# Token sums moved ahead of the switch from a feed-forward to a mixture of experts, on one core

## The chip, the cores and the metric

The kernel runs on one core of a Trainium2 chip. The metric is the device time of one execution in microseconds (us). TensorE is called PE below, VectorE DVE, ScalarE ACT, GpSimd POOL, and SyncE (which issues most DMAs) SP. PEld is the weight load of a PE matmul.

## The reference

A linear attention over 2 x 768 tokens with 8 heads of 48 gives x (1536 x 384). Two layers follow:

```python
h = x @ w_in                                  # 384 -> 2048
g = np.where(h > 0.0, h, np.exp(np.minimum(h, 0.0)) - 1.0)
x = g @ w_out                                 # 2048 -> 384
p = domain_probs / (domain_probs.sum(-1, keepdims=True) + 1e-09)
out = np.zeros((N, D))
for e in range(4):                            # four experts, each 384 -> 1024 -> 384
    out += p[:, e:e + 1] * (np.maximum(x @ w1[e], 0.0) @ w2[e])
```

## The kernel before

All matmuls are made in three passes over operands that are split into a rounded part ("hi") and a remainder ("lo", what the rounding left): hi x hi, hi x lo, lo x hi. Whoever makes an operand for PE therefore makes two: ACT writes hi, and DVE or POOL subtracts it from the full value for lo. A matmul is 128 x 128 by 128 x 512.

**Feed-forward.** The 2048 hidden columns are worked in 48 steps, n = 12 q + 4 block + f, over four quarters q, three blocks of 512 tokens and four groups of 128 columns f. Step n is a set of tokens in a hand-written list, ORDER: `h` (nine matmuls into one PSUM bank, and two ACT operations on it), `e` (DVE reads that bank, line 365, and ACT makes hi), `el` (lo, by DVE for `elnD`, by POOL for `elnP`, line 146 as all remainders of `sub`), `z` (nine matmuls into three banks). After the fourth f, `dr` adds the three banks to x2 (DVE, line 386), and in the last quarter ACT and POOL make hi and lo of x from x2 at once. So dr39 finishes token block 0 of x, dr43 block 1 and dr47 block 2.

**Experts.** The first product of the experts has 16 units of weights (an expert and a pair of its 128-column groups). Units 0 and 1 are made plainly (`plain`, line 564, 12 groups of nine matmuls), from x as it is. Units 2 to 15 take 15 products each in place of 18 (`product`, line 536): sums of token blocks times sums of weight blocks, a bilinear scheme. The sums of weight blocks are made by POOL (`sum_blocks`, line 451) for each unit, six operations, and split by `split_hi` (ACT) and `split_lo` (POOL). The token operands are made once: `sum_tokens` (DVE, line 516, sums of 512-column pieces of x2), then `tokens_hi` (ACT, line 519) and `tokens_lo` (DVE at line 524 where the sign is turned, POOL at line 146 otherwise), which write over places of x that are used up, or into xb. Each product's bank is read by `taken` (DVE line 548, or ACT) into results; chains of products add onto one bank. The hidden values of a group are split by `hidden_hi` (ACT, line 576) and `hidden_lo` (DVE, line 579), and `second` (line 587) multiplies them by the second weights; `weighted` and `added` finish the output.

**The order.** `experts` puts every operation down with a key, and they are emitted in the order of the keys; each engine works its own operations off strictly in that order. A key unit is one piece of three matmuls. The row of pieces is: 36 plain pieces (keys 0 to 35), then 210 products and 288 pieces of `second`, mixed. The end of ORDER (from the sign | on) is put down in front of it with negative keys: an `h` or `z` counts 3. At key 0 the switch closes the pools of the feed-forward (its 8 PSUM banks too) and opens those of the experts: 5 banks for chains and 3 for `second`. Before, all token sums lie behind the switch:

```python
for i, t in enumerate(TOKENS):
    at(1.2 + 1.1 * i, sum_tokens, *t)
...
    k = max(1.9 + 1.1 * made, free + 0.3 + 0.9 * (PLACE[r] // 3))
    at(k, tokens_hi, r)
    at(k + 0.7, tokens_lo, r)
```

The last tokens of ORDER before are "z43 el44D dr43D el39D h45 z44 e45 z39 el45P dr39A e46 h47 z45 el46D z46 e47 el47D z47 dr47A", in the order of PE's parts.

Of the kernel before, what the change touches and what calls it, by code (L numbers as in the profile page):

```python
# [32 lines left out]
TERMS = 18  # L33
EDGE = 120


# [8 lines left out]
HEADS = {0, 6, 3, 9, 14}  # L45
MINUS = {6, 4, 12, 8, 5, 1, 0, 9, 2}

LOADED = [(0, 0), (1, 0), (0, 1), (1, 2), (0, 2), (1, 1)]
W0, W3, W1, W5, W2, W4 = range(5, 11)
SLOT = {11: 0, 0: 1, 8: 2, 9: 3, 14: 4, 7: W0, 2: W3, 3: W2, 6: W4, 4: 11, 10: 12, 13: 13, 5: 14, 12: 15, 1: 16}  # L50

SUMS = [((SLOT[13], SLOT[5]), (W1, W5), "-", (W0, W3)), ((SLOT[4], SLOT[12]), (SLOT[13],) * 2, "-", (W4, SLOT[5])),
        ((SLOT[9], SLOT[10]), (W2, SLOT[5]), "-", (W5, W2)), ((SLOT[11], SLOT[1]), (SLOT[4], SLOT[10]), "+", (W3, W0)),
        ((SLOT[0], SLOT[8]), (W1, W5), "-", (W4, W4)), ((SLOT[14],), (W2,), "-", (W1,))]
PLACE = dict(zip(TURNS, [9, 10, 11, 12, 13, 14, 0, 3, 6, 1, 4, 7, 2, 5, 8]))

TOKENS = [("q", (1, 1), (2, 1)), (0, "q", (0, 1)), (6, (1, 2), None), (3, (2, 2), None), (4, 0, (1, 2)), (7, 4, (0, 2)),
# [3 lines left out]

# [29 lines left out]
def kernel_body(ctx, tc, wkr, vv, uu, w_in, w_out, w1, w2, dp, out):  # L91
# [7 lines left out]
    def feed_forward_pools(es):  # L99
        for name, bufs in (("wpool", 4), ("stage", 4), ("hpool", 3)):  # L100
            pools[name] = es.enter_context(tc.tile_pool(name=name, bufs=bufs))
        pools["psum"] = es.enter_context(tc.tile_pool(name="psum", bufs=8, space=PSUM))

    def bank():
        return pools["psum"].tile([P, 512], F32, tag="bank", name="bank")

    m1 = ExitStack()
    feed_forward_pools(m1)
# [308 lines left out]
    def late_pools(es):  # L417
        for name, bufs in (("w2", 2), ("terms", TERMS), ("hl", 4), ("shares", 4), ("scaled", 4), ("guard", 1)):
            pools[name] = es.enter_context(tc.tile_pool(name=name, bufs=bufs))
        for name, bufs in (("chain", 5), ("second", 3)):  # L420
            pools[name] = es.enter_context(tc.tile_pool(name=name, bufs=bufs, space=PSUM))

    def experts(guard=False, lead=(), switch=None):

        events = []

        def at(key, run, *args):
# [80 lines left out]

        def sum_tokens(name, a, c):
            def of(i):  # L510
                return x2[:, i[0], 512 * i[1]:512 * i[1] + 512] if isinstance(i, tuple) else full[i]
            if c is None:
                full[name] = of(a)
            else:
                full[name] = term()
                nc.vector.tensor_tensor(full[name], of(a), of(c), ALU.add)  # L516
# [4 lines left out]
        def tokens_lo(r):  # L521
            hi, lo = (tokens(r)[:, m] for m in range(2))
            if r in MINUS:
                nc.vector.scalar_tensor_tensor(lo, full[r], -1.0, hi.bitcast(F32), ALU.mult, ALU.subtract)
            else:
                sub("P", lo, full[r], hi)

# [3 lines left out]
        def product(u, r):  # L531
            c = CHAIN[r]
            if r in HEADS:
                banks[c] = pools["chain"].tile([P, 512], F32, tag="chain", name=f"chain_{c}")
            for i, (sa, sm) in enumerate(PASSES):
                nc.tensor.matmul(banks[c], lhsT=weights(u, r, sa), rhs=tokens(r)[:, sm],  # L536
                                 start=r in HEADS and i == 0, stop=i == 2, skip_group_check=True)

        def taken(u, r):
# [10 lines left out]
            if r in (0, 6, 3, 5, 8):  # L550
                copy("A", new({0: 0, 6: 5, 3: 2, 5: 3, 8: 4}[r]), ps)
            elif r == 13:
                op(new(1), ps, y(0), ALU.subtract)
            else:
                o, sign = {4: (2, "-"), 7: (2, "+"), 10: (5, "r"), 12: (0, "-"), 1: (0, "-"), 11: (3, "+"), 9: (3, "r"),
                           14: (1, "+"), 2: (5, "-")}[r]
                a, b = (ps, y(o)) if sign == "r" else (y(o), ps)
                op(y(o), a, b, ALU.add if sign == "+" else ALU.subtract)

        def plain(f, b, j):  # L560
            if j == 0:
                banks["p"] = pools["chain"].tile([P, 512], F32, tag="chain", name="chain_p")
            for i, (sa, sm) in enumerate(PASSES):
# [17 lines left out]
        def second(h, b, f, d):  # L581
            if f == 0:
                k = "chain" if h == 7 and b == 1 else "second"
                sums[d] = pools[k].tile([P, 512], F32, tag=k, name=k)
            w = w2s[h].rearrange("p s (f d) -> p s f d", f=4)
# [46 lines left out]
        row = [("plain", f, b, j) for b in range(3) for f in range(4) for j in range(3)]  # L632
        done = 0
        for n in range(210):
            row.append(("product", 2 + n // 15, TURNS[n % 15]))
            while done < 6 * (n + 1) // 5:
                row.append(("second",) + seconds[done])
                done += 1
# [19 lines left out]
        for e in range(4):  # L658
            for b in range(3):
                at(max(0, place["second", 2 * e, b, 0, 0] - 60), load_share, e, b)  # L660
        for u in range(16):
            n = place["product", u, 0] if u > 1 else -20 + 10 * u
            at(n - 75, load_blocks, u)
            if u < 2:
                for i in (0, 3):
                    at(n - 20 + i, split_hi, u, 0, 5, 6, i, 3)
                    at(n - 19 + i, split_lo, u, 0, 5, 6, i, 3)
                continue
            for i, s in enumerate(SUMS):
                at(n - 50 + 2 * i, sum_blocks, u, *s)  # L670
            for part, first, size, k in ((0, 9, 8, n - 34), (1, 0, 7, n - 14)):
                for i in (0, 4):
                    at(k + i, split_hi, u, part, first, size, i, min(4, size - i))
                    at(k + i + 1.4, split_lo, u, part, first, size, i, min(4, size - i))
        for h in range(8):
            n = place["second", h, 0, 0, 0]
            for m in range(2):
                at(n - 70 + m, load_second, h, m)
                for q in range(2):
                    at(max(0, n - 38 + 6 * m + 3 * q), second_hi, h, m, q)  # L680
                    at(max(0, n - 37 + 6 * m + 3 * q), second_lo, h, m, q)
        for i, t in enumerate(TOKENS):
            at(1.2 + 1.1 * i, sum_tokens, *t)
        for i, r in enumerate(TURNS):
            made = next(j for j, t in enumerate(TOKENS) if t[0] == r)
            free = {0: 11.5, 1: 23.5, 2: 35.5}.get(PLACE[r] % 3, 0) if PLACE[r] < 9 else 0
            k = max(1.9 + 1.1 * made, free + 0.3 + 0.9 * (PLACE[r] // 3))
            at(k, tokens_hi, r)
            at(k + 0.7, tokens_lo, r)
        if guard:  # L690
# [50 lines left out]
    with tc.If(some > 0, preferred_fallthrough_block=False):  # L741
        with ExitStack() as es:
# [80 lines left out]
```

## Time and profile before

| | us |
|---|---|
| runs shown: 679.7, 681.62, 681.14; median | 681.14 |
| profiled execution, device time | 681.25 |
| its span, first to last instruction | 679.4 |
| PE busy in the span | 643.0 |
| DVE busy | 493.6 |
| POOL busy | 403.2 |
| ACT busy | 305.7 |

The profiled execution lies 0.1 us above the median. Device time is its span and 1.85 us around it. The switch lies at about 290 us of the span; the part from there to the end is the experts.

### The profile page before, as it was taken

To read this page: it belongs to the slowest core of one execution; us is meant where nothing else is said; L and a number is where in the kernel's file an instruction comes from. 1 tells how busy PE (TensorE), PEld (TensorE's weight loads), DVE (VectorE), ACT (ScalarE), POOL (GpSimd) and SP (SyncE) were. 2 spreads that over 40 slices of the span, in tenths; PEclk is the share of its full clock that TensorE was granted. 3 is DMA by queue.
4 is the path that set the end of the run, shared out by engine and by line. 5 is a ranking of instruction groups with operands and counts; after the bars stand their busy time and mean duration, and the time that the engine had idled before them with its cause. 6 is when DMAs were issued, how large, how long until landed. Compare 5 with 4: busy or idle time off the path is not lost.

```text
span 679.4 us, 9111 instructions
## 1 busy us (share of the span) xinstructions
PE 643.0 (95%) x3314; PEld 523.8 (77%) x3314; DVE 493.6 (73%) x686; ACT 305.7 (45%) x584; POOL 403.2 (59%) x345
## 2 busy tenths in 40 slices
PE   6977999999999999997999999999999999999994
PEld 4766778888888877874788878878878788788773
DVE  7799998638564753599785787777877868777763
ACT  1334646657565654656444343524443434333220
POOL 5699776435331462787654577765876776744342
PEclk7689999999999999999899999999999999999997
DMA  7575661223202210110202122112130121300012
GB/s 261 163 218 163 189 214 47 69 63 93 70 24 69 78 41 25 69 47 0 86 24 86 32 70 70 39 30 89 40 101 16 40 69 46 103 0 1 0 47 98
DMA packets 20970, 50.83 MB, mean 75 GB/s; under 512 B 2680, under 2 KB 3880, under 8 KB 20916
## 3 DMA queue, kind: packets, MB, share of 16 engines
q1 hardware_dynamic: 20772, 50.15, 23.8%
q8 instruction: 28, 0.46, 0.3%
q14 instruction: 26, 0.21, 0.1%
q10 hardware_dynamic: 144, 0.00, 0.0%
HBM read 46.58 MB, written 2.38 MB: 72 GB/s over the span
## 4 chain that ended last, share of the span: by engine, by line
PE 76%; DVE 12%; POOL 4%; issue 3%; DMA 2%; ACT 2%; SPq 1%; DVEq 0%; POOLq 0%; ACTq 0%
PE second L587 24%; PE bank L357 13%; PE bank L377 12%; PE chain_a L536 8%; PE chain_b L536 5%; PE chain_c L536 3%; DVE terms L516 3%; PE chain_d L536 2%; PE bank L278 2%; PE bank L285 2%; DVE scaled L596 2%; DVE terms L548 1%; PE chain_e L536 1%; PE bank L329 1%; DVE w2s L146 1%
## 5 line engine op out<-in xcount | busy, mean ns | idle before, releaser
L587 PE MATMUL second<-hl,w2s 128*128 128x512 f32 x828 | 223.4, 391 | 4.4 <-DVE hl L579 2.1
L587 PEld LDWEIGHTS second<-hl,w2s 128*128 128x128 f32 x828 | 155.8, 188 | 38.1 <-DVE hl L579 2.4
L601 POOL TENSOR_TENSOR x<-scaled,x 128x512 f32<-128x512 f32 x60 | 84.9, 1437 | 96.1 <-DVE scaled L596 96.1
L146 POOL TENSOR_TENSOR sums<-blocks,sums 128x512 fp32r<-128x512 f32 (+1 forms) x60 | 83.3, 1397 | 36.4 <-ACT sums L150 36.4
L357 PE MATMUL bank<-x,w 128*128 128x512 f32 x432 | 104.1, 391 | 0.4 <-DVE e L365 0.4
L377 PE MATMUL bank<-hl,w 128*128 128x512 f32 x432 | 104.1, 391 | 0.1
L357 PEld LDWEIGHTS bank<-x,w 128*128 128x128 f32 x432 | 80.5, 188 | 18.5 <-DVE e L365 1.4
L377 PEld LDWEIGHTS bank<-hl,w 128*128 128x128 f32 x432 | 80.5, 188 | 17.7 <-POOL hl L146 0.9
L579 DVE SCALAR_TENSOR_TENSOR hl<-terms,hl 128x512 fp32r<-128x512 f32 x96 | 87.6, 916 | 8.0 <-ACT hl L576 7.9
L451 POOL TENSOR_TENSOR blocks<-blocks 128x256 f32<-128x256 f32 x84 | 69.4, 837 | 1.1
L146 POOL TENSOR_TENSOR hl<-e,hl 128x512 fp32r<-128x512 f32 x26 | 35.3, 1361 | 56.2 <-ACT hl L150 56.1
L576 ACT ACTIVATE hl<-terms 128x512 fp32r<-128x512 f32 x96 | 58.1, 624 | 16.3 <-PE chain L587 6.1
L365 DVE SCALAR_TENSOR_TENSOR e<-e,bank 128x512 f32<-128x512 f32 x48 | 32.4, 681 | 40.7 <-ACT e L361 40.7
L536 PE MATMUL chain_a<-x,sums 128*128 128x512 f32 x210 | 60.1, 395 | 1.6 <-DVE terms L548 1.6
L548 DVE TENSOR_TENSOR terms<-terms,chain_a 128x512 f32<-128x512 f32 x42 | 28.7, 683 | 40.0 <-PE chain_a L536 40.0
L150 ACT ACTIVATE sums<-blocks 128x512 fp32r<-128x512 f32 (+1 forms) x60 | 35.4, 593 | 42.2 <-PE chain_b L536 24.9
L150 ACT ACTIVATE terms<-chain_b 128x512 f32<-128x512 f32 x28 | 16.8, 598 | 83.7 <-PE chain_b L536 83.7
L536 PEld LDWEIGHTS chain_a<-x,sums 128*128 128x128 f32 x210 | 39.2, 189 | 11.6 <-DVE terms L548 3.7
L150 ACT ACTIVATE hl<-e 128x512 fp32r<-128x512 f32 x48 | 30.1, 629 | 36.4 <-PE bank L377 24.8
L596 DVE TENSOR_TENSOR scaled<-second,pr 128x512 f32<-128x512 f32 x60 | 39.3, 680 | 5.8 <-PE second L587 5.8
L360 ACT ACTIVATE e<-bank 128x512 f32<-128x512 f32 x48 | 28.4, 592 | 26.3 <-PE bank L357 13.4
L150 ACT ACTIVATE terms<-chain_a 128x512 f32<-128x512 f32 x28 | 16.7, 596 | 48.6 <-PE chain_a L536 48.6
(119 smaller groups left out, 1022.2 us busy)
## 6 DMA issues: line engine op xcount, KB each, us to landing
kr<-in_wkr SPq DMA_DIRECT2D x12, 512.0 KB, 3.9
raw<-in_w_in SPq DMA_DIRECT2D x16, 384.0 KB, 3.6
raw<-in_w_out SPq DMA_DIRECT2D x16, 384.0 KB, 3.2
blocks<-in_w SPq DMA_DIRECT2D x16, 384.0 KB, 3.3
raw<-in_w SPq DMA_DIRECT2D x16, 384.0 KB, 4.3
v<-in_vv SPq DMA_DIRECT2D x12, 456.0 KB, 4.0
w<-in_wkr SPq DMA_DIRECT2D x12, 258.5 KB, 3.8
gw<-in_wkr SPq DMA_DIRECT2D x12, 258.0 KB, 2.8
```

Of the source, the lines that this page charges most:

```text
L146: engines[e].tensor_tensor(o, a, b.bitcast(F32), ALU.subtract)
L150: nc.scalar.activation(out=o, in_=a, func=AF.Copy)
L357: nc.tensor.matmul(ph, lhsT=wi[:, sa, f, kk, :], rhs=x[:, kk, c0:c0 + nch, sm], start=(kk == 0 and i == 0), stop=(kk == 2 and i == 2))
L377: nc.tensor.matmul(pxs[q, bl][d], lhsT=wo[:, sa, f, d * P:(d + 1) * P], rhs=b["t"][:, sm], start=(f == 0 and i == 0), stop=(f == 3 and i = ...
L451: nc.gpsimd.tensor_tensor(*(places(blocks[u], p) for p in (r, a, c)), ALU.subtract if op == "-" else ALU.add)
L536: nc.tensor.matmul(banks[c], lhsT=weights(u, r, sa), rhs=tokens(r)[:, sm], start=r in HEADS and i == 0, stop=i == 2, skip_group_check=True)
L548: nc.vector.tensor_tensor(out, a, b, o)
L576: nc.scalar.activation(out=hls[f, b][:, 0], in_=results[f, b], func=AF.Relu)
L579: nc.vector.scalar_tensor_tensor(hls[f, b][:, 1], results[f, b], 0.0, hls[f, b][:, 0].bitcast(F32), ALU.max, ALU.subtract)
L587: nc.tensor.matmul(sums[d], lhsT=w[:, sa, f, d * P:(d + 1) * P], rhs=hls[4 * h + f, b][:, sm], start=f == i == 0, stop=f == 3 and i == 2)
L596: nc.vector.tensor_tensor(o, sums[d], prs[h // 2, b], ALU.mult)
L601: (nc.vector if last else nc.gpsimd).tensor_tensor(x2[:, d, s], scaled[d], x2[:, d, s], ALU.add)
```

## The change

- TOKENS loses the three entries that only passed a block of x2 on (6, 3 and 14, AS_IS): products 6, 3 and 14 read hi and lo of x as they stand, so `tokens_hi` and `tokens_lo` of these three are gone. Signs (MINUS) are arranged anew, with the signs in `taken` and the sums of weights to match.
- Ten of the sixteen sums that are left (q, 0, s0, 8, s2, v, 9, 12, 1, 11; those that need only token blocks 0 and 1) get the keys -15.5 to -4.7, within the last h and z of the feed-forward, into a pool of their own of 8 buffers; hi and lo of 0, 8, 9, 12, 1 and 11 follow them there. The other six have the keys 0.5 to 6. `tokens_lo` is POOL's for 8, 9 and 12 and DVE's for the other nine.
- The third unit's weights (u = 2): sums at keys -18 to -8 (before -14 to -4), the first half's split from -3 (before 2), the second half's at 32 (before 22). For all units the second half is split 4 keys later, and slots change so that its first user is the ninth product of a unit.
- Six pieces of `second` are put ahead of the first product (AHEAD), which moves that from key 36 to 42; from the thirtieth product on the row is as before.
- The tail of ORDER is changed so that dr39 and dr43 come three h and four z before the switch, with all the `el` there on DVE.
- One pool of 8 PSUM banks serves all stages. The pools of shares, scaled and guard open at key 8 where the ten sums lay, and the first two DMAs of shares move from key 0 to key 9.

```diff
+AHEAD = 6
+SPREAD = 8
-MINUS = {6, 4, 12, 8, 5, 1, 0, 9, 2}
+MINUS = {0, 13, 11, 5, 1}
-SLOT = {11: 0, 0: 1, 8: 2, 9: 3, 14: 4, 7: W0, 2: W3, 3: W2, 6: W4, 4: 11, 10: 12, 13: 13, 5: 14, 12: 15, 1: 16}
+SLOT = {12: 0, 1: 1, 11: 2, 9: 3, 8: 4, 14: 5, 2: W3, 3: W2, 6: W4, 7: W0, 0: 12, 4: 13, 10: 14, 13: 15, 5: 16}
...
+AS_IS = {6: (1, 2), 3: (2, 2), 14: (2, 1)}
+PLACE = {0: 9, 8: 10, 9: 11, 12: 12, 1: 13, 11: 14, 4: 0, 7: 3, 10: 6, 13: 1, 5: 4, 2: 2}
+TOKENS = [("q", (1, 1), (2, 1)), (0, "q", (0, 1)), ("s0", (0, 0), (0, 1)), (8, (1, 0), (1, 1)), ("s2", (2, 0), (2, 1)),
+          ("v", 8, "s2"), (9, "v", "s0"), (12, 8, (2, 1)), (1, 12, "s0"), (11, 12, (0, 1)),
+          (4, 0, (1, 2)), (7, 4, (0, 2)), (10, 9, (2, 2)), (13, "q", (1, 2)), (5, "v", (2, 2)), (2, 10, (0, 2))]
...
-z37 h44 wc31P el42P el43P el38D z41 h39 e44 e39 z42 h46 z38 z43 el44D dr43D el39D h45 z44 e45 z39 el45P dr39A e46 h47
-z45 el46D z46 e47 el47D z47 dr47A
+z37 h39 wc31P el42P el43P el38D z41 e39 h44 z42 z38 e44 el39D z39 el44D dr39D z43 dr43D h45 e45 h46 el45D z44 e46 h47
+el46D z45 e47 z46 el47D z47 dr47A
...
-        for name, bufs in (("w2", 2), ("terms", TERMS), ("hl", 4), ("shares", 4), ("scaled", 4), ("guard", 1)):
+        for name, bufs in (("w2", 2), ("terms", TERMS), ("hl", 4)):
-        for name, bufs in (("chain", 5), ("second", 3)):
-            pools[name] = es.enter_context(tc.tile_pool(name=name, bufs=bufs, space=PSUM))
+    def last_pools(es):
+        for name, bufs in (("shares", 4), ("scaled", 4), ("guard", 1)):
...
+            if r in AS_IS:
+                k, b = AS_IS[r]
+                return x[:, k, 4 * b:4 * b + 4].rearrange("q n s c -> q s n c")
...
-                banks[c] = pools["chain"].tile([P, 512], F32, tag="chain", name=f"chain_{c}")
+                banks[c] = pools["psum"].tile([P, 512], F32, tag="bank", name=f"chain_{c}")
...
-                op(new(1), ps, y(0), ALU.subtract)
+                nc.vector.scalar_tensor_tensor(new(1), ps, -1.0, y(0), ALU.mult, ALU.subtract)
...
+        row += [("second",) + g for g in seconds[:AHEAD]]
...
-                at(n - 50 + 2 * i, sum_blocks, u, *s)
-            for part, first, size, k in ((0, 9, 8, n - 34), (1, 0, 7, n - 14)):
+                at(n - (50 if u > 2 else 60) + 2 * i, sum_blocks, u, *s)
+            for part, at_first, size, k in ((0, 9, 8, n - (34 if u > 2 else 45)), (1, 0, 7, n - 10)):
...
-            at(1.2 + 1.1 * i, sum_tokens, *t)
...
+            made[t[0]] = -15.5 + 1.2 * i if i < 10 else 0.5 + 1.1 * (i - 10)
+            at(made[t[0]], sum_tokens, i < 10, *t)
+        for r, n in PLACE.items():
+            k = max(made[r] + 0.7, {0: 11.5, 1: 23.5, 2: 35.5}[n % 3] + 0.9 * (n // 3) if n < 9 else -99)
             at(k, tokens_hi, r)
-            at(k + 0.7, tokens_lo, r)
+            at(k + 0.9, tokens_lo, "P" if r in (8, 9, 12) else "D", r)
...
+        at(SPREAD, spread_out)
```

## Rows read from the trace of the kernel before

**Rows 1.** Page, part 1 and part 5 (busy, mean ns of one).

```profile
PE 643.0 (95%) x3314; PEld 523.8 (77%) x3314; DVE 493.6 (73%) x686; ACT 305.7 (45%) x584; POOL 403.2 (59%) x345
...
L548 DVE TENSOR_TENSOR terms<-terms,chain_a 128x512 f32<-128x512 f32 x42 | 28.7, 683 | 40.0 <-PE chain_a L536 40.0
```

**Rows 2.** Stretches: length, busy PE, PEld, DVE, ACT, POOL, PE clock, DMA, GB/s.

```profile
270.00:290.00 20.00, 19.85 (x87) 15.78 (x85) 10.61 (x15) 10.93 (x19) 14.37 (x13) 1.00 0.24 79
...
310.00:320.00 10.00, 7.69 (x30) 5.47 (x30) 10.00 (x9) 7.36 (x15) 9.61 (x8) 1.00 0.00 1
320.00:330.00 10.00, 7.18 (x23) 5.56 (x24) 8.06 (x8) 7.50 (x15) 10.00 (x8) 0.83 0.41 144
...
400.00:450.00 50.00, 49.37 (x217) 39.99 (x216) 38.61 (x55) 19.27 (x36) 37.43 (x34) 1.00 0.17 50
```

**Rows 3.** What PE waited for, 230 to 380 us: total, times, longest.

```profile
PE second L587 <- DVE hl L579: 2.1, 1, 2.1
PE chain_p L564 <- ACT terms L150: 1.8, 2, 1.3
PE second L587 <- ACT hl L576: 1.4, 1, 1.4
PE chain_p L564 <- DVE x L386: 0.8, 1, 0.8
```

**Rows 4.** Stretches of 1 us, columns as in Rows 2.

```profile
323.00:324.00 1.00, 0.69 (x3) 0.60 (x4) 1.00 (x2) 1.00 (x3) 1.00 (x1) 0.98 0.00 0
324.00:325.00 1.00, 1.00 (x4) 0.80 (x3) 1.00 (x2) 0.75 (x2) 1.00 (x3) 0.50 0.00 0
...
327.00:328.00 1.00, 1.00 (x5) 0.77 (x5) 0.24 (x1) 0.21 (x1) 1.00 (x1) 0.81 1.05 409
```

**Rows 5.** Timeline of DVE, 290 to 324 us: start, length, operation.

```profile
293.31 1.78 DVE L516 TENSOR_TENSOR terms<-x 128x512 f32<-128x512 f32 x1
...
298.27 0.68 DVE L524 SCALAR_TENSOR_TENSOR x<-terms,x 128x512 fp32r<-128x512 f32 x1
298.87 0.68 DVE L524 SCALAR_TENSOR_TENSOR x<-x,x 128x512 fp32r<-128x512 f32 x1
...
314.08 1.23 DVE L516 TENSOR_TENSOR terms<-terms 128x512 f32<-128x512 f32 x1
```

**Rows 6.** Timeline of POOL, 290 to 324 us.

```profile
296.19 1.74 POOL L146 TENSOR_TENSOR sums<-blocks,sums 128x512 fp32r<-128x512 f32 x1
...
313.57 3.48 POOL L451 TENSOR_TENSOR blocks<-blocks 128x256 f32<-128x256 f32 x3
```

**Rows 7.** Timeline of POOL, 273 to 291 us.

```profile
277.96 3.80 POOL L146 TENSOR_TENSOR x<-x,x 128x512 fp32r<-128x512 f32 x3
...
288.36 2.93 POOL L451 TENSOR_TENSOR blocks<-blocks 128x256 f32<-128x256 f32 x4
```

**Rows 8.** The chain that ended last, 260 to 400 us: start, length.

```profile
267.11 2.05 PE bank L377 x9
```

**Rows 9.** Timeline of DVE, 273 to 291 us.

```profile
273.96 2.05 DVE L386 TENSOR_TENSOR x<-bank,x 128x512 f32<-128x512 f32 x3 [3.40 <-PE bank L377]
...
278.65 0.69 DVE L365 SCALAR_TENSOR_TENSOR e<-e,bank 128x512 f32<-128x512 f32 x1 [1.53 <-ACT e L361]
```

**Rows 10.** Timeline of PE, 268 to 292 us.

```profile
271.04 4.24 PE L377 MATMUL bank<-hl,w 128*128 128x512 f32 x18
275.12 2.20 PE L357 MATMUL bank<-x,w 128*128 128x512 f32 x9
```

**Rows 11.** Timeline of ACT, 273 to 291 us.

```profile
277.36 0.60 ACT L360 ACTIVATE e<-bank 128x512 f32<-128x512 f32 x1
277.99 0.63 ACT L361 ACTIVATE e<-e 128x512 f32<-128x512 f32 x1
```

**Rows 12.** What PE waited for, 380 to 680 us.

```profile
PE chain_a L536 <- DVE terms L548: 1.6, 5, 0.3
...
PE second L587 <- DVE scaled L596: 0.9, 1, 0.9
```

More of the change, by code (lines that the diff above doesn't have):

```diff
@@ L417, in late_pools @@
     def late_pools(es):
-        for name, bufs in (("w2", 2), ("terms", TERMS), ("hl", 4), ("shares", 4), ("scaled", 4), ("guard", 1)):
+        for name, bufs in (("w2", 2), ("terms", TERMS), ("hl", 4)):
             pools[name] = es.enter_context(tc.tile_pool(name=name, bufs=bufs))
-        for name, bufs in (("chain", 5), ("second", 3)):
-            pools[name] = es.enter_context(tc.tile_pool(name=name, bufs=bufs, space=PSUM))
+    def last_pools(es):
+        for name, bufs in (("shares", 4), ("scaled", 4), ("guard", 1)):
+            pools[name] = es.enter_context(tc.tile_pool(name=name, bufs=bufs))
     def experts(guard=False, lead=(), switch=None):
         events = []
+        first, last = ExitStack(), ExitStack()
+        pools["first"] = first.enter_context(tc.tile_pool(name="first", bufs=8, side="right"))
         def at(key, run, *args):
@@ L507, in term, with sum_tokens, tokens_lo @@
             return pools["terms"].tile([P, 512], F32, tag="terms", name="terms")
-        def sum_tokens(name, a, c):
+        def sum_tokens(early, name, a, c):
             def of(i):
                 return x2[:, i[0], 512 * i[1]:512 * i[1] + 512] if isinstance(i, tuple) else full[i]
[L512 to L516, printed above, removed]
+            full[name] = pools["first"].tile([P, 512], F32, tag="first", name="first") if early else term()
+            nc.vector.tensor_tensor(full[name], of(a), of(c), ALU.add)
         def tokens_hi(r):
             nc.scalar.activation(out=tokens(r)[:, 0], in_=full[r], func=AF.Copy, scale=-1.0 if r in MINUS else 1.0)
-        def tokens_lo(r):
+        def tokens_lo(e, r):
             hi, lo = (tokens(r)[:, m] for m in range(2))
@@ L525, in tokens_lo @@
             else:
-                sub("P", lo, full[r], hi)
+                sub(e, lo, full[r], hi)
         results, banks = {}, {}
@@ L550, in taken @@
             if r in (0, 6, 3, 5, 8):
-                copy("A", new({0: 0, 6: 5, 3: 2, 5: 3, 8: 4}[r]), ps)
+                nc.scalar.activation(out=new({0: 0, 6: 5, 3: 2, 5: 3, 8: 4}[r]), in_=ps, func=AF.Copy, scale=-1.0 if r in (6, 8) else 1.0)
             elif r == 13:
-                op(new(1), ps, y(0), ALU.subtract)
-            else:
-                o, sign = {4: (2, "-"), 7: (2, "+"), 10: (5, "r"), 12: (0, "-"), 1: (0, "-"), 11: (3, "+"), 9: (3, "r"),
-                           14: (1, "+"), 2: (5, "-")}[r]
+                nc.vector.scalar_tensor_tensor(new(1), ps, -1.0, y(0), ALU.mult, ALU.subtract)
+            elif r == 9:
+                nc.vector.scalar_tensor_tensor(y(3), ps, -1.0, y(3), ALU.mult, ALU.subtract)
+            else:
+                o, sign = {4: (2, "+"), 7: (2, "+"), 10: (5, "r"), 12: (0, "+"), 1: (0, "-"), 11: (3, "-"),
+                           14: (1, "+"), 2: (5, "+")}[r]
                 a, b = (ps, y(o)) if sign == "r" else (y(o), ps)
@@ L561, in plain @@
             if j == 0:
-                banks["p"] = pools["chain"].tile([P, 512], F32, tag="chain", name="chain_p")
+                banks["p"] = pools["psum"].tile([P, 512], F32, tag="bank", name="chain_p")
             for i, (sa, sm) in enumerate(PASSES):
@@ L582, in second @@
             if f == 0:
-                k = "chain" if h == 7 and b == 1 else "second"
-                sums[d] = pools[k].tile([P, 512], F32, tag=k, name=k)
+                sums[d] = pools["psum"].tile([P, 512], F32, tag="bank", name="second")
             w = w2s[h].rearrange("p s (f d) -> p s f d", f=4)
@@ L632, in experts @@
         row = [("plain", f, b, j) for b in range(3) for f in range(4) for j in range(3)]
-        done = 0
+        row += [("second",) + g for g in seconds[:AHEAD]]
+        done = AHEAD
         for n in range(210):
             row.append(("product", 2 + n // 15, TURNS[n % 15]))
-            while done < 6 * (n + 1) // 5:
+            while done < (AHEAD + (36 - AHEAD) * (n + 1) // 30 if n < 30 else 6 * (n + 1) // 5):
                 row.append(("second",) + seconds[done])
@@ L659, in experts @@
             for b in range(3):
-                at(max(0, place["second", 2 * e, b, 0, 0] - 60), load_share, e, b)
+                at(max(SPREAD + 1, place["second", 2 * e, b, 0, 0] - 60), load_share, e, b)
         for u in range(16):
@@ L665, in experts @@
                 for i in (0, 3):
-                    at(n - 20 + i, split_hi, u, 0, 5, 6, i, 3)
-                    at(n - 19 + i, split_lo, u, 0, 5, 6, i, 3)
+                    at(n - 20 + i, split_hi, u, 0, 6, 6, i, 3)
+                    at(n - 19 + i, split_lo, u, 0, 6, 6, i, 3)
                 continue
             for i, s in enumerate(SUMS):
-                at(n - 50 + 2 * i, sum_blocks, u, *s)
-            for part, first, size, k in ((0, 9, 8, n - 34), (1, 0, 7, n - 14)):
+                at(n - (50 if u > 2 else 60) + 2 * i, sum_blocks, u, *s)
+            for part, at_first, size, k in ((0, 9, 8, n - (34 if u > 2 else 45)), (1, 0, 7, n - 10)):
                 for i in (0, 4):
-                    at(k + i, split_hi, u, part, first, size, i, min(4, size - i))
-                    at(k + i + 1.4, split_lo, u, part, first, size, i, min(4, size - i))
+                    at(k + i, split_hi, u, part, at_first, size, i, min(4, size - i))
+                    at(k + i + 1.4, split_lo, u, part, at_first, size, i, min(4, size - i))
         for h in range(8):
@@ L681, in experts, with spread_out @@
                     at(max(0, n - 37 + 6 * m + 3 * q), second_lo, h, m, q)
+        made = {}
         for i, t in enumerate(TOKENS):
-            at(1.2 + 1.1 * i, sum_tokens, *t)
[L684 to L687, printed above, removed]
-            at(k, tokens_hi, r)
-            at(k + 0.7, tokens_lo, r)
+            made[t[0]] = -15.5 + 1.2 * i if i < 10 else 0.5 + 1.1 * (i - 10)
+            at(made[t[0]], sum_tokens, i < 10, *t)
+        for r, n in PLACE.items():
+            k = max(made[r] + 0.7, {0: 11.5, 1: 23.5, 2: 35.5}[n % 3] + 0.9 * (n // 3) if n < 9 else -99)
+            at(k, tokens_hi, r)
+            at(k + 0.9, tokens_lo, "P" if r in (8, 9, 12) else "D", r)
+        def spread_out():
+            first.close()
+            last_pools(last)
+        at(SPREAD, spread_out)
         if guard:
@@ L698, in experts @@
                 run(*args)
+        last.close()
     early, late = ExitStack(), ExitStack()
@@ L709, in kernel_body @@
     early.close()
+    m0.close()
     def recur(i, gp):
```

22 lines of the change are left out of this document (12 added, 10 removed), and 3 rows, old and new, of the table TOKENS.

## The prediction

> **What bounds the kernel now.** I read the page first: PE is busy 643.0 of 679.4 us [rows 1], so a change that leaves PE's work as it is can win or lose only where PE stands idle or runs on a lower clock. The stretches say where. In steady state (400 to 450 us) PE is busy 49.37 of 50 us, and DVE and POOL 38.6 and 37.4; around the switch, from 310 to 330 us, it loses 5.1 us of 20, while DVE is busy 10.00 of 10 and POOL 9.61 to 10.00 [rows 2]. Third, the waits of PE there: four entries, 2.1 + 1.8 + 1.4 + 0.8 = 6.1 us, the longest of them for a remainder of hidden values on DVE, one for an ACT that itself stands behind token sums, and 0.8 us at the switch for the last adds into x2 [rows 3]. Fourth, the clock: after these gaps the granted clock falls from 1.00 to 0.50 (2.4 to 1.2 GHz) at about 324 us and is back during the microsecond from 327 on [rows 4]; 3.5 us at half speed cost 1.8 us. So what the stage at the switch can give back is 6.1 + 1.8 = 7.9 us, 1.2% of the time.
>
> **Why DVE is late there.** The timelines of DVE and POOL, read side by side, show the price of a token sum. Where POOL is idle, two DVE remainders start at 298.27 and 298.87, so one takes 0.60 us. Where POOL works, a token sum takes 1.78 us and one beside 256-column sums 1.23 us [rows 5], and POOL's operations stretch as well: a 512-column remainder takes 1.74 us, three block sums 3.48 us, 1.16 each [rows 6], while without a two-input operation of DVE beside them POOL takes 3.80 / 3 = 1.27 us and 2.93 / 4 = 0.73 us [rows 7]. That is a pair taking turns: 1.74 us for one DVE and one POOL operation of 512 columns, 1.16 us with a block sum. I book DVE's 0.60 us and put the rest on POOL: 1.14 us for 512 columns, 0.56 us for a block sum. What DVE reads from PSUM is not held: the adds into x2 take 2.05 / 3 = 0.68 us and `e` 0.69 us, the adds with POOL at work for part of the time [rows 9]. So in both stages DVE and POOL share a budget, and what counts is the sum of their operations on SBUF.
>
> The Trainium skill, SBUF — State Buffer, section Who interferes with whom, says that a DVE instruction with two SBUF inputs and a GpSimd instruction that reads SBUF exclude each other, and that the second one to issue waits until the first has finished. By that rule a pair of 512 columns costs 1.27 + 0.60 = 1.87 us, not the 1.74 us of the rows; over the six pairs of that size below this would be 0.8 us more (an estimate from that page and the rows): 687 in place of 686.
>
> **The change, part by part.** *The plain stretch (keys 0 to 36) gets lighter.* Ten of sixteen sums leave it, with three remainders of DVE and all three of POOL's that are left; the three tokens read as they are take three ACT operations and three POOL or DVE operations out for good. What is left for DVE: six sums, four remainders of the second weights, six of tokens, two of hidden values, 18 x 0.60 = 10.8 us, and three adds. POOL has three remainders of block 2, one half of unit 2, the block sums of unit 3 and two more halves: 6 x 1.14 + 6 x 0.56 = 10.2 us. Together 21 us in the 24.5 us that 36 pieces of 0.68 us take (nine matmuls take 2.05 us [rows 8]), and the first product, which needs a token, is six pieces later still. All four waits of [rows 3] have lost their cause, and PE does not stand long enough there for the clock to fall: -6.1 and -1.8 us.
>
> *The feed-forward's tail gets the ten sums.* Here is the cost, and the key list gives it. I count t from the start of z43, nine matmuls 2.05 us: h45 ends at t = 4.1, h46 at 6.1, z44 at 8.2, h47 at 10.2, z45 at 12.2; z46 is due then, and z47 at 14.3. DVE's queue is in order. The adds of dr39 and dr43 start with the first finished bank (before: 273.96 us, within the z pair that PE ran from 271.04 to 275.28 [rows 9, 10]), so they are done at about t = 3. Then e45 waits for h45 and two ACT operations, 0.60 and 0.63 us [rows 11], and ends at about t = 6.2; the first sum, q, stands behind it (keys -18 and -15.5). From there to el47 DVE has, in this order: q, el45, 0, s0, lo of 0, e46, 8, s2, v, el46, 9, 12, e47, 1, 11, lo of 1, lo of 11, el47. Sixteen of these read SBUF twice: 9.6 us. POOL, which makes hi's remainders for blocks 0 and 1 from t = 0.2 on at 1.27 us each, has two of six left at t = 6.3, then six block sums of unit 2 (five of 256 columns, one of 128, taken at 0.4), the remainders of 8, 9 and 12, and a half of unit 2: 6 x 1.14 + 5 x 0.56 + 0.4 = 10.0 us. A few tenths of that run beneath e46 and e47, which read PSUM. So el47 is done at t = 6.3 + 9.6 + 10.0 - 0.4 = 25.5, and z47, due at 14.3, starts 11.2 us late. The first third of it appears already at z46: up to el46 there are nine DVE operations (5.4 us), two POOL remainders and four block sums (4.5 us), t = 16.2 against 12.2, less what POOL waits for ACT. PE can't work ahead, since z46 and z47 stand in front of the plain pieces. A gap of this length is longer than the one that halved the clock before [rows 4]: +1.8 us. Queued behind el47 are dr47 and the remainders of second weights, which nobody needs for 36 pieces.
>
> Bounds: with POOL not in the way at all, DVE needs 6.3 + 16 x 0.60 + two at 0.69 and el47 is done at t = 17.4, 3.1 us late, too short for the clock; with the page's rule 12.0 us late. I take the pair prices, because the rows show them over nearly the whole stage at the switch, and POOL has a full queue in the tail too (14.37 of 20 us before, DVE 10.61 [rows 2], and now unit 2's sums come 4 keys earlier and the remainders of three tokens on top).
>
> *Other edits, at nothing.* The second halves of a unit's weights come 4 keys later but are first needed 17 pieces into the unit; if that cover were gone, it would show as a wait like the 0.9 us one below. A subtraction with a sign in `taken` is DVE's one read of PSUM as before (0.683 us, and `e` in the other form 0.69 [rows 1, 9]). The DMAs of shares move from key 0 to 9 on SP's queue, 40 pieces or 27 us ahead of their first use, and the loads behind them (block weights, second weights) have keys 19 and up. From the thirtieth product on the row is the same. The common PSUM pool can take away the 1.6 us that chains wait and the 0.9 us of a `second` [rows 12], or add such waits where a bank just read is handed out next: -2.5 to a few us; I take 0.
>
> Sum, against the profiled execution's own 681.25 us (0.1 above the median, so I leave it): 681.25 - 6.1 - 1.8 + 11.2 + 1.8 = 686.35, said as 686.
>
> **The rivals.** (1) Forecast: the tail is overbooked, 686, its own range 683.5 to 689.5. (2) The other side: DVE and POOL do not collide in the tail, because POOL waits for ACT's hi there (it does so before each token remainder) and DVE runs at 0.60 us. Then el47 is 3.1 us late and the sum is 681.25 - 7.9 + 3.1 = 676.4. For it speaks that remainders of DVE ran at 0.60 while POOL waited [rows 5]; against it that POOL has at t = 6.3 two remainders and block sums in front of it that wait for nobody. It decides for faster from the point where el47 is done before t = 14.3 + 6.1 = 20.4 or, if the clock stays up, 22.2. (3) In between, about half of the collisions: el47 at t = 21 to 22.5, 681 or so, no measurable change. (4) The common banks hand PE a bank that DVE has still to read, once per unit at 0.3 to 0.9 us [rows 12]: 14 units, 4 to 13 us on top, 690 to 699; nothing in the rows shows such a wait at the feed-forward's eight banks. (5) The change doesn't do what it says: DVE comes out of the tail so late that the plain stretch waits as before. Then nothing is won back, 681.25 + 11.2 = 692.5; against it speak the 3.5 us of slack above and six more pieces.
>
> **How the numbers follow.** Chances: (1) 0.58, (2) 0.20, (3) 0.13, (4) and (5) 0.09 together. About 0.3%, 2 us, is what a measurement of this kernel can tell from no change. (1) is slower throughout; (2) gives faster; (3) is split, most of it no change, with 0.02 to either side; so faster 0.22, same 0.11, slower 0.67. The range reaches from (2)'s 676 over all of (1) to 690, and leaves out (4), (5) and part of (2)'s lower side, where banks also save 2.5 us.
>
> **What would show it.** In the changed kernel PE should wait for DVE's `hl` of line 146 (el46, el47) just before the plain pieces, some 3 and 8 us, with DVE's token sums there at 1.2 to 1.8 us and the granted clock at 0.50 as the plain pieces begin; the waits of [rows 3] should be gone, and the stretch after the switch full. I am wrong if those sums run at 0.60 to 0.70 us, if PE's two waits add up to less than 6 us, or if new waits for banks stand in the steady part.

## The result and the profile after

The changed kernel takes 685.17 us (684.47 to 687.3, 8 runs), the kernel before in the same runs 681.1 us (679.7 to 682.98, 8 runs). The ratio is 1.0065, 95% interval 1.0048 to 1.0082: slower by 4.1 us, and by more than the 0.3% that a measurement of this kernel can tell. The profiled execution of the changed kernel took 684.58 us, its span 682.6 us, 3.3 and 3.2 us more than before.

First what PE waited for in the changed kernel from 230 to 380 us, which answers to [rows 3]:

```profile
PE bank L384 <- DVE hl L153: 7.8, 3, 4.8
PE bank L384 <- ACT hl L157: 2.4, 2, 1.2
PE chain_b L547 <- DVE terms L559: 0.5, 1, 0.5
PE bank L364 <- DVE e L372: 0.5, 2, 0.3
```

All four waits of before are gone: no plain piece waits for ACT or for x2, no `second` for hidden values. In their place stand waits of the feed-forward's z (line 384 now) for its hi and lo, 10.2 us. The stretches, which answer to [rows 2], show where: PE is short from 270 to 300 us and on half its clock from 290 on, and the stretch that was short before, from 310 to 330 us, is full.

```profile
270.00:290.00 20.00, 15.80 (x68) 12.27 (x67) 17.09 (x21) 11.04 (x19) 15.80 (x13) 1.00 0.15 51
290.00:300.00 10.00, 4.04 (x10) 2.45 (x9) 8.93 (x8) 3.63 (x6) 6.67 (x6) 0.52 0.00 0
300.00:310.00 10.00, 10.00 (x37) 7.98 (x37) 7.34 (x8) 5.57 (x11) 8.15 (x7) 0.80 0.01 2
310.00:320.00 10.00, 10.00 (x46) 8.29 (x45) 6.96 (x9) 4.24 (x9) 3.67 (x4) 1.00 0.25 79
320.00:330.00 10.00, 10.00 (x46) 8.29 (x45) 3.37 (x5) 6.83 (x14) 1.64 (x2) 1.00 0.00 1
```

The timeline of PE there gives each wait its place (start, length, operation, idle time before it and what ended it): z39 and z43, then h45 and h46, z45, and z46 and z47, each with its first matmul (hi) apart from the eight that follow.

```profile
271.99 4.15 PE L384 MATMUL bank<-hl,w 128*128 128x512 f32 x17 [1.64 <-DVE hl L153]
275.97 4.24 PE L364 MATMUL bank<-x,w 128*128 128x512 f32 x18
...
284.13 2.20 PE L384 MATMUL bank<-hl,w 128*128 128x512 f32 x9
287.52 0.49 PE L384 MATMUL bank<-hl,w 128*128 128x512 f32 x1 [1.19 <-ACT hl L157]
289.39 2.94 PE L384 MATMUL bank<-hl,w 128*128 128x512 f32 x8 [1.37 <-DVE hl L153]
293.50 0.79 PE L384 MATMUL bank<-hl,w 128*128 128x512 f32 x1 [1.17 <-ACT hl L157]
299.08 3.78 PE L384 MATMUL bank<-hl,w 128*128 128x512 f32 x8 [4.79 <-DVE hl L153]
```

z46 waits 2.6 us and z47 6.0 us. h45 starts at 275.97, so z43, nine matmuls, had started at 273.9; z47's second matmul, the first to read lo, was due 64 matmuls after that, at 288.4, and came at 299.08: 10.7 us late, the two waits and the slower matmuls of z46 together. What DVE did in that time, by its timeline: the first sum q, el45, the sums 0 and s0, and further down v, el46, the sum 9, the sum 11 and el47.

```profile
280.11 0.95 DVE L527 TENSOR_TENSOR first<-x 128x512 f32<-128x512 f32 x1
280.99 1.78 DVE L153 TENSOR_TENSOR hl<-e,hl 128x512 fp32r<-128x512 f32 x1
282.69 1.22 DVE L527 TENSOR_TENSOR first<-first,x 128x512 f32<-128x512 f32 x1
283.83 1.23 DVE L527 TENSOR_TENSOR first<-x 128x512 f32<-128x512 f32 x1
...
288.04 0.69 DVE L527 TENSOR_TENSOR first<-first 128x512 f32<-128x512 f32 x1
288.65 0.68 DVE L153 TENSOR_TENSOR hl<-e,hl 128x512 fp32r<-128x512 f32 x1
289.25 1.80 DVE L527 TENSOR_TENSOR first<-first 128x512 f32<-128x512 f32 x1
...
294.20 1.75 DVE L527 TENSOR_TENSOR first<-first,x 128x512 f32<-128x512 f32 x1
...
297.26 1.77 DVE L153 TENSOR_TENSOR hl<-e,hl 128x512 fp32r<-128x512 f32 x1
```

There is hardly a gap, and the prices are the two of before: 1.7 to 1.8 us beside a 512-column operation of POOL, 1.2 us beside a block sum, 0.68 where POOL had nothing to do. From 286.8 to 289.2 us POOL waited for ACT's hi of token 8:

```profile
282.18 4.62 POOL L465 TENSOR_TENSOR blocks<-blocks 128x256 f32<-128x256 f32 x4
289.21 1.29 POOL L153 TENSOR_TENSOR x<-first,x 128x512 fp32r<-128x512 f32 x1 [2.42 <-ACT x L530]
```

The granted clock, microsecond by microsecond, as in [rows 4]:

```profile
289.00:290.00 1.00, 0.61 (x3) 0.52 (x4) 1.00 (x2) 0.14 (x1) 0.79 (x1) 1.00 0.00 0
290.00:291.00 1.00, 1.00 (x5) 0.82 (x4) 1.00 (x2) 0.00 (x0) 1.00 (x2) 0.70 0.00 0
...
303.00:304.00 1.00, 1.00 (x4) 0.72 (x3) 0.59 (x1) 0.38 (x1) 1.00 (x2) 0.50 0.08 16
304.00:305.00 1.00, 1.00 (x6) 0.83 (x5) 0.30 (x1) 1.00 (x3) 1.00 (x2) 0.97 0.00 0
```

It is at 0.50 (1.2 GHz) from the middle of z46 until 304 us.

**Where the 3.3 us of the profiled executions come from.** The chain that ended last gives three fixed places. The second h of the feed-forward's last tail starts at 264.74 us before and 263.71 after, 1.0 us earlier. The difference is already there in the attention, whose code is the same: a group of 16 matmuls that starts at 59.58 us before starts at 58.45 after. The product of chain d that stands at 414.74 before stands at 419.36 after, so the stage from the tail to there costs 5.6 us more (150.00 us before, 155.65 after). The last small matmul, at 656.08 before, is at 659.61 after, so 1.1 us comes back in the steady part, where the 0.9 us of a `second` [rows 12] is gone and the 1.6 us of the chains is still there. From the first of these places to the last the changed kernel takes 4.6 us more (391.3 us before, 395.9 after), near the 4.1 us by which the medians differ.

### The profile page after: what moved, and what is told of

It reads as the page before. It is cut to its first block, busy times and chain, and to the rows that moved or that the text cites. A ratio compares the mean times of both kernels' runs of the same rounds, so it can differ in the third digit from the quotient of the medians.

```text
span 682.6 us, 9079 instructions
## 1 busy us (share of the span) xinstructions
PE 641.2 (94%) x3314; PEld 521.6 (76%) x3314; DVE 498.1 (73%) x687; ACT 304.0 (45%) x581; POOL 397.4 (58%) x341
## 4 chain that ended last, share of the span: by engine, by line
PE 77%; DVE 10%; POOL 5%; issue 3%; DMA 2%; ACT 1%; SPq 0%; DVEq 0%; POOLq 0%; ACTq 0%
PE second L599 25%; PE bank L364 12%; PE bank L384 12%; PE chain_a L547 8%; PE chain_b L547 4%; PE chain_p L577 4%; PE chain_c L547 3%; PE chain_d L547 3%; DVE scaled L608 2%; DVE first L527 2%; PE bank L292 1%; PE chain_e L547 1%; PE bank L285 1%; POOL kr L150 1%; PE bank L336 1%
## 5 line engine op out<-in xcount | busy, mean ns | idle before, releaser
L599 PE MATMUL second<-hl,w2s 128*128 128x512 f32 x864 | 230.5, 389 | 0.0
L599 PEld LDWEIGHTS second<-hl,w2s 128*128 128x128 f32 x864 | 162.0, 188 | 34.1 <-DVE hl L592 0.2
L384 PE MATMUL bank<-hl,w 128*128 128x512 f32 x432 | 107.8, 400 | 10.2 <-DVE hl L153 7.8
L153 POOL TENSOR_TENSOR sums<-blocks,sums 128x512 fp32r<-128x512 f32 (+1 forms) x60 | 81.3, 1366 | 55.5 <-ACT sums L157 55.5
L384 PEld LDWEIGHTS bank<-hl,w 128*128 128x128 f32 x432 | 81.9, 192 | 29.9 <-DVE hl L153 9.0
L592 DVE SCALAR_TENSOR_TENSOR hl<-terms,hl 128x512 fp32r<-128x512 f32 x96 | 90.6, 947 | 13.3 <-ACT hl L589 13.3
L465 POOL TENSOR_TENSOR blocks<-blocks 128x256 f32<-128x256 f32 x84 | 70.9, 861 | 1.7 <-DMA blocks<-in_w 0.6
L547 PE MATMUL chain_a<-x,sums 128*128 128x512 f32 x168 | 47.2, 389 | 0.0
L608 DVE TENSOR_TENSOR scaled<-second,pr 128x512 f32<-128x512 f32 x63 | 41.2, 679 | 7.5 <-PE second L599 7.5
L547 PEld LDWEIGHTS chain_a<-x,sums 128*128 128x128 f32 x168 | 31.5, 188 | 6.5
```

Source lines behind the costliest of these rows:

```text
L153: engines[e].tensor_tensor(o, a, b.bitcast(F32), ALU.subtract)
L384: nc.tensor.matmul(pxs[q, bl][d], lhsT=wo[:, sa, f, d * P:(d + 1) * P], rhs=b["t"][:, sm], start=(f == 0 and i == 0), stop=(f == 3 and i = ...
L465: nc.gpsimd.tensor_tensor(*(places(blocks[u], p) for p in (r, a, c)), ALU.subtract if op == "-" else ALU.add)
L592: nc.vector.scalar_tensor_tensor(hls[f, b][:, 1], results[f, b], 0.0, hls[f, b][:, 0].bitcast(F32), ALU.max, ALU.subtract)
L599: nc.tensor.matmul(sums[d], lhsT=w[:, sa, f, d * P:(d + 1) * P], rhs=hls[4 * h + f, b][:, sm], start=f == i == 0, stop=f == 3 and i == 2)
L608: nc.vector.tensor_tensor(o, sums[d], prs[h // 2, b], ALU.mult)
```

## The experiments

Each was run beside the kernel before, and the ratio is to that. Theory A is the prediction's: the ten sums overbook the tail, taking turns with POOL, in front of el46 and el47 in DVE's queue.

**All sums behind the switch.**

```diff
-            made[t[0]] = -15.5 + 1.2 * i if i < 10 else 0.5 + 1.1 * (i - 10)
-            at(made[t[0]], sum_tokens, i < 10, *t)
+            made[t[0]] = 1.2 + 1.1 * i
+            at(made[t[0]], sum_tokens, False, *t)
```

> The changed kernel with all sixteen token sums put back behind the switch (keys 1.2 + 1.1 i), all else as changed. Theory A (the ten sums overbook the tail, taking turns with POOL in front of el46 and el47): PE's waits at z46 and z47 (8.5 us with the clock at 0.50 after them) are gone; DVE has 31 operations in the plain stretch again, but three remainders fewer on POOL and six pieces more time, so it is at most 3 to 5 us late there: 678, between 676 and 681. Rival C (the new order of the feed-forward's last steps, with all remainders on DVE, costs the time, not the sums): the waits at z46 and z47 stay, 684 to 686.

Measured: 678.42 us, ratio 0.9962 (0.9942 to 0.9982). The longest waits of this kernel from 230 to 380 us:

```profile
PE second L599 <- ACT hl L589: 3.8, 1, 3.8
PE bank L384 <- DVE hl L153: 1.6, 1, 1.6
```

z46 and z47 do not wait, so the sums cost the tail, not its order. Only the wait at z39 stays, the one part of rival C that holds. With the sums behind the switch PE waits there instead, 3.8 us for the first hidden values. The rest of the change, taken as a whole, is worth a gain of 0.4%; which of its other edits it comes from (the three tokens read as they are, the six pieces put ahead, the banks, the slots) no run tells apart, but for the banks below.

**POOL's other work out of the tail, the ten sums in it.**

```diff
-                at(n - (50 if u > 2 else 60) + 2 * i, sum_blocks, u, *s)
-            for part, at_first, size, k in ((0, 9, 8, n - (34 if u > 2 else 45)), (1, 0, 7, n - 10)):
+                at(n - (50 if u > 2 else 40) + 2 * i, sum_blocks, u, *s)
+            for part, at_first, size, k in ((0, 9, 8, n - (34 if u > 2 else 28)), (1, 0, 7, n - 10)):
...
+            if r in (8, 9, 12):
+                k = {8: 2, 9: 3, 12: 4}[r]
```

> The changed kernel, its ten early sums in place, but POOL's other work taken out of the tail: unit 2's block sums at keys 2 to 12 and its first half split at 14 and 18, hi and lo of tokens 8, 9 and 12 at keys 2 to 5. Theory A (turn-taking with POOL): from the first sum on DVE meets two POOL operations in place of twelve, el47 is done some 5.6 us earlier (9.6 us of its own, 2.3 us of POOL, 1.4 us for e46 and e47), 679.5, and 676 to 677 if the clock then stays up. Rival B (DVE's own number of operations is the cost, POOL does not matter): the token sums still take as long as they do, no change, 684 to 686.

Measured: 677.35 us, ratio 0.9955 (0.9931 to 0.9979). The timeline of DVE there, POOL's two neighbouring entries, and PE at z46 and z47:

```profile
284.47 0.68 DVE L527 TENSOR_TENSOR first<-first,x 128x512 f32<-128x512 f32 x1
285.07 0.68 DVE L527 TENSOR_TENSOR first<-x 128x512 f32<-128x512 f32 x1
...
290.19 0.68 DVE L527 TENSOR_TENSOR first<-first,x 128x512 f32<-128x512 f32 x1
...
294.10 0.68 DVE L153 TENSOR_TENSOR hl<-e,hl 128x512 fp32r<-128x512 f32 x1
```

```profile
275.99 8.02 POOL L153 TENSOR_TENSOR x<-x,x 128x512 fp32r<-128x512 f32 x6 [0.78 <-ACT x L157]
...
297.05 4.12 POOL L153 TENSOR_TENSOR x<-x,x 128x512 fp32r<-128x512 f32 x3 [13.05 <-ACT x L157]
```

```profile
289.72 2.11 PE L384 MATMUL bank<-hl,w 128*128 128x512 f32 x8 [1.34 <-DVE hl L153]
292.19 0.50 PE L384 MATMUL bank<-hl,w 128*128 128x512 f32 x1 [0.36 <-ACT hl L157]
294.84 2.11 PE L384 MATMUL bank<-hl,w 128*128 128x512 f32 x8 [2.15 <-DVE hl L153]
```

With POOL idle for 13 us the sums from 0 on take 0.68 us, z47's remainder comes 2.15 us after PE is ready for it and not 4.79, and the clock stays at 1.00. Rival B, that POOL does not matter and the time stays at 684 to 686, falls. DVE's own work, with the two remainders of POOL that are left beside q and el45, still keeps PE waiting at z46 and z47 for 1.34 + 0.36 + 2.15 = 3.9 us of the 8.5; the rest of the waits and the half clock came with POOL's work. The time is close to that of the prediction's rival of no collisions (676.4), reached by taking most of the collisions away.

**Three early sums, where DVE idles.**

```diff
-SPREAD = 8
+SPREAD = 24
...
-            made[t[0]] = -15.5 + 1.2 * i if i < 10 else 0.5 + 1.1 * (i - 10)
-            at(made[t[0]], sum_tokens, i < 10, *t)
+            made[t[0]] = [-18.8, -18.6, -16.5, -2.8, -2.6, -2.4][i] if i < 6 else 0.6 + 1.3 * (i - 6)
+            at(made[t[0]], sum_tokens, i < 6, *t)
...
+            if r == 0:
+                k = -17
             at(k, tokens_hi, r)
-            at(k + 0.9, tokens_lo, "P" if r in (8, 9, 12) else "D", r)
+            at(-11.5 if r == 0 else k + 0.9, tokens_lo, "P" if r in (8, 9, 12) else "D", r)
```

> The changed kernel with only three early sums: q and 0 between dr43 and e45, where DVE idles, s0 behind e45; s2, 8 and v directly behind el47, the other ten after the switch; the pools of shares open at key 24. Theory A: up to el47 DVE has seven operations on SBUF, and el45, el46 and el47 are ready within a few tenths of when z45, z46 and z47 are due, so PE waits at most 1 us before the switch; after it DVE has 13 sums in 42 pieces and is just in time: 676, between 674.5 and 678. Rival B (own count) says the same here; rival C (the order of the last steps): 682 or more.

Measured: 674.27 us, ratio 0.9914 (0.9882 to 0.9945), just below the range that was expected. z46 and z47 do not wait; what is left are two waits of 1.3 us and more:

```profile
PE bank L384 <- DVE hl L153: 1.6, 1, 1.6
PE second L599 <- ACT hl L589: 1.3, 1, 1.3
```

**The single pool of banks alone**, in the kernel before.

```diff
-        for name, bufs in (("chain", 5), ("second", 3)):
-            pools[name] = es.enter_context(tc.tile_pool(name=name, bufs=bufs, space=PSUM))
...
-                banks[c] = pools["chain"].tile([P, 512], F32, tag="chain", name=f"chain_{c}")
+                banks[c] = pools["psum"].tile([P, 512], F32, tag="bank", name=f"chain_{c}")
...
```

> The kernel before with one thing of the change, the single pool of 8 PSUM banks. If the banks matter: the 0.8 us at the switch, the 1.8 us that plain pieces waited for ACT behind token sums, and the 0.9 us of a second product go, 678 to 680. If they are handed out too soon after a read, waits of 0.3 us and more per unit: 682 or more. If neither, 681.

Measured: 678.62 us, ratio 0.9972 (0.9947 to 0.9996). The waits of the plain pieces are gone, and so is the 0.9 us of the steady part. What is gained in the plain stretch is given back at once, since DVE and POOL are no earlier than before: from 230 to 380 us the waits add up to 6.9 us, against 6.8 before. The three largest are

```profile
PE chain_d L537 <- POOL sums L149: 3.3, 1, 3.3
PE second L587 <- DVE hl L580: 1.7, 1, 1.7
PE second L587 <- ACT hl L577: 1.5, 1, 1.5
```

Between the second h of the tail and the last small matmul this kernel takes 1.3 us less than before (390.0 us for 391.3), 0.9 us of it the `second`. The gain in the medians is 2 us, and its interval nearly reaches no change.

**Two mends on the kernel with three sums.** PE waited at z39 because el39 stood behind e44 in DVE's queue, which waits for ACT; and POOL, whose keys hold nothing back, ran unit 3's block sums beside DVE's last token sums.

```diff
-z37 h39 wc31P el42P el43P el38D z41 e39 h44 z42 z38 e44 el39D z39 el44D dr39D z43 dr43D h45 e45 h46 el45D z44 e46 h47
+z37 h39 wc31P el42P el43P el38D z41 e39 h44 z42 z38 el39D e44 z39 el44D dr39D z43 dr43D h45 e45 h46 el45D z44 e46 h47
...
-                at(n - (50 if u > 2 else 60) + 2 * i, sum_blocks, u, *s)
-            for part, at_first, size, k in ((0, 9, 8, n - (34 if u > 2 else 45)), (1, 0, 7, n - 10)):
+                at(n - (50 if u > 3 else 38 if u == 3 else 60) + 2 * i, sum_blocks, u, *s)
+            for part, at_first, size, k in ((0, 9, 8, n - (34 if u > 3 else 25 if u == 3 else 45)), (1, 0, 7, n - 10)):
```

> The kernel with three early sums, and two places mended that its trace still showed: el39 goes ahead of e44 on DVE (PE waited 1.6 us for it at z39), and unit 3's block sums go behind the second half of unit 2's weights on POOL, since they ran at 1.06 us each beside DVE's token sums, twelve pairs before the first hidden values were due (PE waited 1.3 + 0.2 us). If DVE's queue order and the turns with POOL set these waits, 671.5, between 670 and 673; if the 1.6 us only move to the next wait, 674.

Measured: 671.22 us (669.29 to 671.44), ratio 0.9842 (0.9818 to 0.9866): the lowest time of the study, with two versions below close to it. Both waits are gone; this is what PE still waited for from 230 to 380 us:

```profile
PE chain_b L547 <- DVE terms L559: 0.5, 1, 0.5
PE bank L364 <- DVE e L372: 0.5, 2, 0.3
PE bank L384 <- DVE hl L153: 0.2, 1, 0.2
```

**The ten sums, but behind el47.**

```diff
-            made[t[0]] = -15.5 + 1.2 * i if i < 10 else 0.5 + 1.1 * (i - 10)
+            made[t[0]] = -2.9 + 0.1 * i if i < 10 else 0.5 + 1.1 * (i - 10)
```

> The changed kernel with the same ten early sums in the same pool, POOL's work as changed, and one thing different: the sums stand behind el47 on DVE (keys -2.9 to -2.0) and not between e45, e46 and e47. Theory A says that the cost lies in who is queued behind them: z46 and z47 wait no more, and the sums run from the time of z47 on; DVE then has some 3 us more than with all sums behind the switch, 676, between 674.5 and 678. If the ten sums cost the stage the same wherever they stand before the plain pieces (the shared budget alone), 681 or more.

Measured: 680.74 us, ratio 0.9977 (0.9957 to 0.9996). A miss: I expected 676, between 674.5 and 678. The runs spread from 677.5 to 683.0 us, and the profiled one (682.37) is among the longest. The tail behaves as theory A says, with no wait at z46 or z47, but PE then waited 4.5 us for the first remainder of hidden values, and the granted clock fell behind it (a mean of 0.66 from 320 to 330 us). In the timeline of POOL, beside DVE's last token sums, and in PE's waits:

```profile
310.11 6.37 POOL L465 TENSOR_TENSOR blocks<-blocks 128x256 f32<-128x256 f32 x6
```

```profile
PE second L599 <- DVE hl L592: 4.5, 1, 4.5
```

So the lateness had moved past the switch. The next three runs, with the two mends of above on three placements, tell whether DVE's own work or these block sums made it late.

**Ten sums behind el47, with the mends.**

> The ten sums behind el47, with the two mends (el39 ahead of e44; unit 3's block sums behind the second half of unit 2 on POOL). The run without the mends missed its number: 680.7, its tail without waits, but 4.5 us of waiting for the remainder of the first hidden values, with POOL's six block sums of unit 3 beside DVE's last token sums for 6.4 us. If that collision made DVE late, the mends take it away: 1.6 us of z39 and most of 4.5 us and of the low clock after it, 673.5, between 672 and 675. If DVE is late by its own number of operations, only the 1.6 us go: 679.

Measured: 671.86 us, ratio 0.9862 (0.984 to 0.9883), just below the range that was expected; that wait is gone, and so is the one at z39. The collision with the block sums made DVE late: had it been DVE's own number of operations, 679 was expected. The two mends were made together; what each is worth alone is not shown.

**All sums behind the switch, with the mends.**

> All sixteen sums behind the switch, with the two mends. Says what the three early sums of the best version are worth by themselves: it waits 3.8 us for hidden values without the mends, and the block sums' share of that goes: 674, between 672.5 and 676. If the mends were all that mattered, it is at 671 like the version with three early sums.

Measured: 672.11 us, ratio 0.9877 (0.9855 to 0.9899), again just below the range that was expected. By the medians it lies 0.9 us above the version with three early sums, by the ratios 0.35%, 2.4 us, and the intervals of the ratios overlap; between the second h of the tail and the last small matmul the two traces take 382.4 and 381.6 us. What early sums are worth by themselves is not settled: about 1 us by the traces and the medians.

**The changed kernel, with the mends.**

> The changed kernel, its ten sums in the tail in front of el46 and el47, with the two mends. Theory A: the waits at z46 and z47 and the clock after them stay, only the 1.6 us at z39 go: 683.5, between 682.5 and 685. If the plain stretch was the true cause, it comes near the others, under 678.

Measured: 684.41 us (682.67 to 685.67), ratio 1.0052 (1.0034 to 1.007). The wait at z39 is gone, and those at z46 and z47 stay:

```profile
PE bank L384 <- DVE hl L153: 7.0, 2, 5.1
PE bank L384 <- ACT hl L157: 2.3, 2, 1.7
```

The place of ten sums, and of the hi and lo that follow them, in the queues therefore makes the difference between 684.4 and 671.9 us, with the same operations.

## Why the prediction was right, step by step

*The forecast, slower, 686.0 us against 685.17.* The mechanism is the one that was named, and each link of it was shown on its own: the sums are the cause (all behind the switch: 678.4), POOL is what makes them long (POOL quiet: 677.4 with the sums at 0.68 us), and their standing in front of el46 and el47 is what makes PE wait (behind el47 and mended: 671.9; in front and mended: 684.4). That the number came so close is in part luck, as the next paragraphs show.

*What the stage gives back, 6.1 us of waits and 1.8 us of clock.* Right: none of the four waits is there, and the clock is at 1.00 from 310 to 330 us. The slack that I gave the plain stretch (21 us of work in 24.5, unit 3's block sums among it) held: PE had itself been held up until el47 was done, so DVE was not behind when the plain pieces began, and after its last sums there it waited 4.07 us for ACT.

*The walk through DVE's queue.* I had q at t = 6.3, el46 at 16.2 less what POOL waits, and el47 at 25.5. With z43 at 273.9 us, q began at t = 6.2, el46 ended at 15.4 and el47 at 25.1. z47 was 10.7 us late against 11.2. The "less" was real: POOL waited for ACT's hi of token 8, and v and el46 ran at 0.6 to 0.7 us. But the sum for el47, 6.3 + 9.6 + 10.0 - 0.4, leaves out the time of e46 and e47 themselves, 1.4 us, which its own lower bound (el47 at 17.4) has; with them it would have said 26.9 and a kernel of 687.7 us. And it booked too much for POOL: of the 18.9 us from q to the end of el47, DVE's sixteen operations make 9.6 and e46 and e47 1.4, which leaves 7.9 us for the turns with POOL, where the sum had 9.6. The two mistakes, 1.4 us too little and 1.7 us too much, nearly cancel; that el47 came within 0.4 us is luck, its being late by about 11 us is not.

*The turns.* Sums took 1.75 to 1.80 us beside a 512-column operation and 1.22 beside a block sum, as before. The Trainium skill, SBUF — State Buffer, section Who interferes with whom, is borne out in kind by the quiet run (1.8 us with POOL, 0.68 without). By its full wait a pair would take 1.87 us (an estimate, 1.27 + 0.60 from the rows before); the rows say 1.74.

*The clock.* I had one fall worth 1.8 us behind z47. It fell earlier, within z46, and 7.7 us of PE's busy time ran at half clock, which loses 3.9 us; of these, z46's share is hidden beneath DVE's lateness. The bound with POOL not in the way took a z47 that is 3.1 us late as too short for the clock; the two waits behind which it fell here were 1.19 and 1.37 us, while in the quiet run, with z47 4.6 us late, it stayed at 1.00.

*What I had not seen.* The wait of 1.6 us at z39: I began the walk at z43 and took the tokens ahead of it as free, while the new ORDER had put el39 behind an e44 that waits for ACT. The waits at z46 and z47, the clock, z39 and a new wait of 0.5 us of chain b add up to 8.5 + 3.9 + 1.6 + 0.5 = 14.5 us, for 11.2 + 1.8 = 13.0 predicted. Less the 7.9 us given back that is 6.6 us, against 5.6 between the two fixed places. The waits of 0.3 us and less that this leaves out are 0.8 us before and 0.5 after, which brings it to 6.3; the last 0.7 us is not traced. That the profiled execution is 1.0 us earlier before any edit, and takes 1.1 us less in the steady part (I took 0, with a bound of 2.5 for the banks), makes most of the way from 5.6 to the 3.3 us; the first of these is no work of the change.

*The rivals.* That the sums do not collide was wrong for this kernel, and near in size once POOL was quiet (677.4 for 676.4, though el47 was done at t = 19.0 there, not at 17.4, and z39's 1.6 us came on top). Banks handed out too soon did not show: alone the single pool measures 0.3% faster, at the limit of what can be told. That the plain stretch stays late was wrong for the changed kernel, and was what I ran into myself with the sums behind el47: the same collision, moved on.

## What to carry to other kernels

In these traces a DVE operation with both inputs in SBUF and a POOL operation take turns (1.7 to 1.8 us for a sum beside a 512-column operation, 0.68 us alone), so a stage in which both have work has one budget, and idle time of DVE in front of a switch is worth only what POOL leaves of it there. An in-order queue counts twice: look at what stands behind the moved work on its engine and when PE needs that, and place filler behind the operation that PE is waiting for, or where the engine idles for its inputs. Keys hold nothing back: an engine runs ahead to whatever is ready, so work that must not collide has to stand behind something that is late.

## What the runs showed of the hardware that I had not expected

PE's clock fell to 0.50 after two waits of 1.19 and 1.37 us with one matmul between them (287.52 us in the changed kernel), but stayed at 1.00 in the run with POOL quiet, through waits of 1.34, 0.36 and 2.15 us that had nine matmuls between the first and the last of them. And the first 50 us, whose code is the same in all these kernels, ran at a mean granted clock of 0.77 in the profiled execution before, 0.88 in that of the changed kernel and 0.90 with the banks alone. The 1 us by which the profiled executions differ before any edit may have to do with it, but the clock does not settle it: with the ten sums behind el47 that stretch ran at 0.86, and the second h of the tail came at 266.34 us, later than the 264.74 before. In the eleven traces this place lies anywhere from 262.88 to 266.34 us, so a few us between two single profiles say nothing until such a place has been subtracted.
